# First batch of an attention, gated-MLP and expert-attention kernel: half a q/k tile behind packed scores and weights, bias split earlier, w_o conversion later

## The chip, the cores and the metric

The kernel runs on one core of a Trainium2 chip. The metric is device time in microseconds (us), the median of a few executions. TensorE (PE) does the matmuls, VectorE (DVE), ScalarE (ACT) and GpSimd (POOL) the elementwise work, and SyncE (SP) issues nearly all DMAs.

## The reference

Three stages follow each other for each of 8 batches of 576 tokens.

```python
p_packed = sm_attn(p, k, v)               # 32 packed queries a head, 8 heads, head_dim 64
attn = sm_attn(q, p_packed, p_packed)     # 576 queries a head over the 32 packed rows
x = attn.transpose(0, 2, 1, 3).reshape(B, S, 512)
h = gelu(x @ w_in); u, v = split(h)       # 512 and 512 columns
v_n = layernorm(v) * g_ln
v_s = w_sg @ v_n + b_sg                   # over the 576 tokens
x = x + (u * v_s) @ w_out
# experts: 4 heads of 64 with causal attention, each weighted by a top-2 gate
out = sum_e gate_e(x) * softmax(causal(x wq_e (x wk_e)^T)) (x wv_e) wo_e
```

## The kernel before

**Precision.** Most matmuls run three times (`PASSES`) on operands split into a high and a low part. `act_copy` makes a high part on ACT, `lo_part` the low one on DVE or POOL, both by helpers, so that all of them stand on L83 and L86.

**Two folds.** `w_out` is multiplied into the expert weights (`fold`), so q and k of the experts are made from two sources: the gated part `g` against the folded `w_qk` (`qk_gated`, 24 matmuls a tile), and the attention's own output, whose packed rows are first multiplied with `w_qk` and `w_vg` head by head (`bdw_qk`, `bdw_vg`: 16 matmuls each, giving `bdq` and `bdv`) and then used by `qk_packed` and `vlog`. The weights for `bdw_qk` and `bdw_vg` are other copies than the folded ones: they come by DMA from `kept_qk` and `kept_vg` (L204, L197).

**Order.** `startup()` runs a list of names, `ORDER`, that prepares the weights and the first batch; all engines follow that list there. In it `Dbias` loads `b_sg`, `bi` (`bias_high`, one ACT copy) and `bj` (`bias_low`, four DVE instructions, L304 to L308) split it. After it come, for the first batch, `first_back(0)` and the rest of the batch's second half, then batch by batch a front (MLP) beside the back of the batch ahead. PE and SP take their instructions in the order in which the program writes them. DVE and ACT are placed by a scheduler, except within `manual_schedule` blocks.

**The next batch's keys.** `join("k", j)` interleaves two 16-bit planes (`kp`, loaded from `turned_k`) into a key tile `kT`, two POOL copies for each of four tiles. `make_pT` (L467) transposes the packed queries; `s0` and `s1` are the packed scores (L398), each followed by an exp (`a`, L501). `a0`, `a1` transpose the results (a1T), `pp` multiplies them with v, `P0`, `P1` copy the transposed packed rows (ppT, L446) for the second attention (s with qT, L398), whose result meets `w_in` (wp).

**w_o.** `load_w_o` (L360) loads the experts' output weights; `prep_w_o` converts them, one ACT copy (L83) and one DVE instruction for each of two halves. It is written in `later_back(1)`, and the scheduler places it in the first batch.

Of the kernel before, what the change touches and what calls it, by code (L numbers as in the profile page):

```python
# [26 lines left out]
def packed_attention_mlp_moe_kernel(  # L27
# [18 lines left out]
    nc = tc.nc  # L46
# [44 lines left out]
    ET = mybir.EngineType  # L91
# [293 lines left out]
    STEP = {}  # L385
# [62 lines left out]
    def p1_steps(b):  # L448
# [39 lines left out]
        def join(name, j):  # L488
            t = s.pop((name + "p", j))
            o = slot("D", name=name + "T")  # L490
            w = o.bitcast(U16).rearrange("p (n i) -> p i n", i=2)
            for i in range(2):
                nc.gpsimd.tensor_copy(w[:, i], t[:, i].rearrange("p h n -> p (h n)"))  # L493
            s[name, j] = two(o)

        def s1(Q):
# [67 lines left out]
        last = None  # L564
        for name, src in (("k", k), ("q", q)):
            for j in range(4):
                TURN.append([lambda a=last: a and keep(*a), lambda a=(name, src, j): turn(*a)])
                last = (name, j)
# [14 lines left out]

        STEP[b, "f"] = f_
        if b == 1:
            STEP[b, "fk"], STEP[b, "fv"] = fk_, fv_

        def K(Q):
            if Q == 0:
                make_pT()  # L590
            for j in (2 * Q, 2 * Q + 1):
                join("k", j)
                planes("q", j)

        def Q_(Q):
# [85 lines left out]
    def bdw_qk(b):  # L681
        s = ST[b]
        pt = pd("bdq")
        per_head(b, pt, 512, w_of(b, "qk"))
        for Q in range(2):
            s["bd", Q] = [slot("B", F32R, 512, name="bdq") for _ in range(2)]
            nc.scalar.activation(s["bd", Q][0], pt[:, Q, :], AF.Copy)
        for Q in range(2):
            hi, lo = s["bd", Q]
            lo_part(nc.vector, lo, pt[:, Q, :], hi)  # L690

    def bdw_vg(b):
# [103 lines left out]
    def two(t):  # L796
        return t.rearrange("p (h n) -> p h n", h=2)
# [80 lines left out]
        qk_gated(b, i, True)  # L878
        qk_packed(b, i, False)

    def qk_gated(b, i, first, ms=range(4)):
        s = ST[b]
        if first:
            s["qkp", i] = pd("qk")[:, :, :HALF]
        o = s["qkp", i]
        cols = slice(i * P, (i + 1) * P)
        for m in ms:
            for x, y in PASSES:
                for h in range(2):
                    nc.tensor.matmul(o[:, h, :], W["w_qk"][y][:, m, cols], s["g", m][x][:, hs(h)],  # L890
                                     start=first and (m, x, y) == (0, 0, 0), stop=not first and (m, x, y) == (3, 1, 0))

    def qk_packed(b, i, first):
        s = ST[b]
# [10 lines left out]
    def qk_out(b, i):  # L905
        qk_high(b, i)
        qk_low(b, i)
# [526 lines left out]
    def first_back(b, do_all):  # L1434
        tick(len(TURN))
        do_all("V K0")
        qk_gated(b, 0, True)
        do_all("K1")
        with tc.manual_schedule(engines={ET.DVE}):
            do_all("s0 s1")  # L1440
            bdw_qk(b)
            do_all("n0 n1")
            qk_gated(b, 2, True)
            qk_packed(b, 0, False)
            do_all("a0 a1")
            qk_out(b, 0)
            bdw_vg(b)
            weights(b + 1, ("in1", "in0"))
            qk_packed(b, 2, False)
            qk_out(b, 2)  # L1450
        keep_last_q(b, 0)
        gate_beside(b)
        do_all("pp Q0 Q1")
        vlog(b, VT[2])
        do_all("P0 P1")
        vlog(b, VT[1])
        second(b + 1, do_all)
        load_w_o()
        ahead(b + 2)

    def later_back(b, go, do_all, nxt):
        with tc.manual_schedule(engines={ET.DVE}):
            go("N0 N2")
            vs_tile(b, 0)
        vs_mm(b, 1)
        with tc.manual_schedule(engines={ET.Activation}):
            go("T0 T2")
            vs_out(b, 1)
        vs_tile(b, 2)
        go("y0 y1")  # L1470
        if b == 1:
            for j in range(2):
                prep_w_o(j)
        go("S5 S4")
        vs_tile(b, 3)
        tick(len(TURN))
        if b + 1 < B:
            STEP.pop((b + 1, "f"))()
        with tc.manual_schedule(engines={ET.DVE, ET.Activation}):
            go("o0 T5 T4 o1 y2")  # L1480
            bdw_vg(b)
            bdw_qk(b)
            go("E6 E7 N6 N7")
        weights(b + 1, ("in1", "in0"))
        qk(b, 0)
        do_all("V o2 T6 T7 K0 S8 S9 K1")
        keep_last_q(b, 0)
        gate_beside(b)
        qk_gated(b, 2, True)
        qk_packed(b, 2, False)  # L1490
        qk_high(b, 2)
        with tc.manual_schedule(engines={ET.DVE}):
            do_all("s0 s1")
# [12 lines left out]
    def back(b, go):
        def do_all(names):

            for n in names.split():
                if (b + 1, n) in STEP:  # L1510
                    STEP.pop((b + 1, n))()
                elif n[0] in "STyo":
                    go(n)

        nxt = attention(b)
        if b:
            later_back(b, go, do_all, nxt)
        else:
            first_back(b, do_all)
        if b + 1 == B:  # L1520
            return
        vlog(b, VT[0])
        tick()
        gates(b)
        qk_packed(b, 1, True)
        qk_packed(b, 3, True)
        qk_gated(b, 1, False)
        qk_out(b, 1)
        keep_last_q(b, 1)
        tick()  # L1530
        qk_gated(b, 3, False)
        tick()
        qk_out(b, 3)
        weights(b + 1, ("qk", "vg"))
        return nxt

# [4 lines left out]
    def first():  # L1541
# [189 lines left out]
        for c in range(4):  # L1731
# [10 lines left out]
            Dwsg=lambda: [load_w_sg(c) for c in range(NT)])  # L1742
# [24 lines left out]
        for m in range(4):  # L1767
            for n, fn in (("vk", vs_keep), ("u", u_mm), ("ug", u_gelu), ("go", gate_mul), ("gh", gate_high), ("gl", gate_low)):
                Z[f"{n}{m}"] = lambda fn=fn, m=m: fn(0, m)
        put(ki1=lambda: keep_w_in(1), ki0=lambda: keep_w_in(0), A=lambda: ahead(1), t=tick,  # L1770
            F=lambda: STEP.pop((1, "fk"))(), Fv=lambda: STEP.pop((1, "fv"))(), Wq=load_first_qk,
            W=lambda: weights(0, ("vg",)))
        for i, (o, x) in enumerate(keep_w_steps()):
            Z[f"kw{i}"] = lambda o=o, x=x: nc.sync.dma_start(o, x)
# [1 line left out]

    ORDER = """
        Dwo3 Dwo1 wo3t wo3p Dwo0 Din12 wo1t Dk1 wo3L K1 wo1a wo1p in12t in12a wo1L Kc1 wo0t wo1g Dwo2 wo0p wo2t Dk0
        wo3a wo3g K0 Dp wo0a pT pTc wo0L in12p Dwsg s1 wo0g Din10 in12l Kc0 sm1 se1 wo2p in12g w3 s0 Dq1 ar1 Din13
        sm0 wh3 wv3 aT1 aTc1 se0 Qn1 in10t Dv1 wo2a n1 aT0 Qc1 in10p in13t wo2l w2 wo2g w0 in13p pp1 wH2 aTc0 in13l  # L1780
        n0 wH0 Dq0 ppc1 ppT1 ppTc1 wT1 wL2 S1 Dv0 ar0 wTc1 in10a Qn0 wL0 pp0 in13a St1 Sx1 in10l in13g Din11 wl3 Qc0
        ppc0 in10g in11t wT3 wTc3 in11p w1 ppT0 wT2 w4 Ss1 Dfqk ppTc0 in11l S0 wTc2 Se1 St0 Su1 in11a Sx0 Ss0 wH4
        Dfvg Din00 wh1 Sn1 wv1 Sb1 fa1 ah1 fb1 in11g Se0 wL4 A wp1 fh1 Su0 Sn0 t Sb0 fa2 kw0 wph1 al1 in00t ah0 al0
        Din02 kw1 t wT0 wpl1 fl1 Dbias Dgbc Din03 kw2 v0 Din01 v1 in03t in02t wTc0 t in03p kw3 v2 in03a bi g1 in03l
        g0 bj kw4 in00a wl1 b0 fb2 ki1 b1 kw5 v3 c0 fh2 t in02p pw1 in02a kw6 g2 pw0 c1 b2 g3 in02l vh0 kw7 t pw2
        vh1 c2 kw8 vh2 in03g v4 vl0 b3 fa0 c3 t x4 fb0 fl2 kw9 fh0 in00p y4 vl1 kw10 fl0 pw3 in00l t vl2 g4 b4 vs1_0
        c4 kw11 pw4 vs0_0 vs1_1 vs0_1 vs3_0 vs3_1 in02g vH3 t in01t vs0_2 vs1_2 kw12 vs2_0 vL3 vs3_2 vH4 in01a vL4
        in01p kw13 vs0_3 t vs0_4 in00g in01L vk0 vs3_3 kw14 in01g vs2_1 vs2_2 ki0 wp0 kw15 wph0 vs2_3 vs1_3 kw16
        vs3_4 vs1_4 wpl0 vs2_4 kw17 vk2 u2 u0 ug2 kw18 go2 ug0 go0 u1 kw19 u3 gh2 ug1 F Wq Fv gh0 fa3 gl2 gl0 fb3 W vk1
        go1 vk3 ug3 go3 gh1 gh3 gl1 gl3 fh3 fl3  # L1790
    """

    def startup():
# [42 lines left out]
```

## Time and profile before

| | |
|---|---|
| median of three runs | 797.6 us (797.13 to 800.81) |
| profiled execution, own time | 800.65 us |
| span of its instructions | 798.9 us |
| mean granted PE clock | 0.994 |
| PE / DVE / ACT / POOL busy | 97% / 73% / 53% / 28% |
| DMA moved | 114.05 MB, 143 GB/s |

The profiled execution is 3.05 us above the median. Its time holds 1.75 us beyond the span. Positions below are us from the start of the span. `startup()` reaches to about 98 us, and the first batch's back, with most of the change in it, to about 142 us.

### The profile page before, as it was taken

The numbers are of one execution on the slowest core, as the hardware profiler recorded it, in microseconds if no ns is written. First come the engines' busy times: TensorE is split into PE (matmuls) and PEld (weight loads), VectorE is DVE, ScalarE is ACT, GpSimd is POOL, SyncE is SP. The second block draws the span as 40 slices with busy tenths as digits, with TensorE's granted clock in tenths as the row PEclk, the third lists the DMA queues.
The fourth block names the chain that finished last, engine by engine and source line by source line (L and its number), as shares of the span: only waits on it lengthen the run. The fifth ranks groups of instructions, "written<-read, shape, count | busy, mean of one in ns | idle before, by whom it ended". The sixth has DMA issues, their size and how long they took to land.

```text
span 798.9 us, 18875 instructions
## 1 busy us (share of the span) xinstructions
PE 772.3 (97%) x7361; PEld 682.8 (85%) x7361; DVE 580.2 (73%) x1316; ACT 425.6 (53%) x949; POOL 220.8 (28%) x337
## 2 busy tenths in 40 slices
PE   3899998999999999999999999999999999999998
PEld 1567887998899888998799898998899898998987
DVE  7699447876588767886588766886589676886493
ACT  3665424665347553666357463666347563566365
POOL 1346242315232332304232332304232331400000
PEclk9899999999999999999999999999999999999999
DMA  9997899528382656629283655619273562001002
GB/s 291 263 243 183 190 295 196 144 66 259 68 204 75 196 142 163 156 61 264 76 201 83 160 171 164 161 47 269 66 208 96 130 195 101 1 2 41 1 15 66
DMA packets 169268, 114.05 MB, mean 143 GB/s; under 512 B 115738, under 2 KB 150042, under 8 KB 166492
## 3 DMA queue, kind: packets, MB, share of 16 engines
q1 hardware_dynamic: 169180, 112.86, 53.5%
q8 instruction: 58, 0.95, 0.5%
q14 instruction: 30, 0.25, 0.1%
HBM read 68.26 MB, written 29.63 MB: 123 GB/s over the span
## 4 chain that ended last, share of the span: by engine, by line
PE 89%; DMA 5%; DVE 3%; SPq 1%; issue 1%; ACT 0%; DVEq 0%; ACTq 0%
PE vs L836 13%; PE qk L890 13%; PE qk L902 6%; PE u L806 6%; PE y L1222 6%; PE vlog L963 5%; PE o L1271 5%; PE v L716 5%; PE aTp L1176 3%; PE sc L1047 3%; PE vlog L967 3%; PE s L398 2%; DMA raw_in<-in_moe_w_in_dram 2%; PE wp L636 2%; PE sc L1135 2%; PE sc L1078 1%
## 5 line engine op out<-in xcount | busy, mean ns | idle before, releaser
L890 PE MATMUL qk<-g,w_qk 128*128 128x288 f32 x768 | 107.0, 297 | 0.4 <-ACT a L501 0.4
L890 PEld LDWEIGHTS qk<-g,w_qk 128*128 128x128 f32 x768 | 103.2, 188 | 4.1 <-issue 2.7
L836 PE MATMUL vs<-w_sg,vnh 128*128 128x288 f32 x512 | 90.9, 299 | 1.0 <-DVE w_vg L86 1.0
L836 PEld LDWEIGHTS vs<-w_sg,vnh 128*128 128x128 f32 x512 | 74.6, 188 | 4.8 <-issue 2.1
L1066 ACT ACTIVATE at<-sc,nm 128x384 f32<-128x384 f32 (+3 forms) x72 | 43.3, 607 | 41.6 <-DVE nm L1055 38.8
L83 ACT ACTIVATE aT<-aTp 128x512 f32<-128x512 f32 (+4 forms) x125 | 54.6, 514 | 17.5 <-PE aTp L1106 12.4
L932 POOL CAST g<-g 128x64 fp32r<-128x64 f32 x32 | 10.0, 316 | 168.9 <-DVE g L86 126.3
L836 PE MATMUL vs<-w_sg,vnl 128*128 128x288 f32 x256 | 54.8, 296 | 0.2 <-POOL vnl L86 0.2
L1222 PEld LDWEIGHTS y<-aT,v 128*64 128x64 f32 (+1 forms) x960 | 45.1, 137 | 10.0 <-issue 3.6
L1222 PE MATMUL y<-aT,v 128*64 128x128 f32 (+2 forms) x960 | 52.0, 259 | 0.0
L963 PE MATMUL vlog<-w_vg,g 128*128 128x260 f32 x384 | 52.0, 284 | 0.0
L752 POOL TENSOR_TENSOR rstd<-rstd,mhalf 128x1 f32<-128x1 f32 (+1 forms) x40 | 35.2, 882 | 60.2 <-DVE rstd L748 50.3
L963 PEld LDWEIGHTS vlog<-w_vg,g 128*128 128x128 f32 x384 | 48.4, 189 | 1.1 <-PE wp L636 0.9
L1271 PE MATMUL o<-w_o,y 128*128 128x512 f32 x186 | 48.9, 399 | 0.0
L493 POOL COPY qT<-qp 128x576 uint16<-128x576 uint16 x56 | 44.8, 868 | 13.6 <-DMA qp<-turned_q 13.5
L493 POOL COPY kT<-kp 128x576 uint16<-128x576 uint16 x56 | 43.3, 842 | 14.2 <-PE sc L1047 8.3
L86 DVE TENSOR_TENSOR y<-y 128x256 fp32r<-128x256 f32 (+1 forms) x40 | 15.8, 396 | 42.7 <-ACT y L1248 42.3
L902 PE MATMUL qk<-a2h,bdq 128*128 128x288 f32 x256 | 44.6, 296 | 0.0
L912 ACT ACTIVATE qk<-qk 128x576 fp32r<-128x576 f32 x32 | 20.8, 651 | 41.9 <-PE qk L890 22.0
L836 PEld LDWEIGHTS vs<-w_sg,vnl 128*128 128x128 f32 x256 | 41.1, 188 | 0.4 <-POOL vnl L86 0.4
L927 POOL CAST last_q<-qk 64x64 fp32r<-64x64 f32 x64 | 14.9, 232 | 94.6 <-ACT aT L83 40.4
L548 POOL TENSOR_TENSOR bt<-bt,mx 128x576 f32<-128x576 f32 x14 | 16.2, 1159 | 86.8 <-DVE mx L547 86.8
(267 smaller groups left out, 1916.4 us busy)
## 6 DMA issues: line engine op xcount, KB each, us to landing
w_in<-kept_in SPq DMA_DIRECT2D x14, 1024.0 KB, 7.2
turned_k<-kx SPq DMA_DIRECT2D x28, 288.0 KB, 2.6
turned_q<-qx SPq DMA_DIRECT2D x28, 288.0 KB, 2.4
kp<-turned_k SPq DMA_DIRECT2D x56, 144.0 KB, 3.0
qp<-turned_q SPq DMA_DIRECT2D x56, 144.0 KB, 3.1
out_dram<-ot SPq DMA_DIRECT2D x31, 256.0 KB, 2.1
v<-in_v_dram SPq DMA_DIRECT2D x56, 128.0 KB, 4.7
w_qk<-kept_qk SPq DMA_DIRECT2D x7, 1024.0 KB, 6.6
```

The source lines that it names most:

```text
L83: nc.scalar.activation(o, i, AF.Copy, scale=scale)
L493: nc.gpsimd.tensor_copy(w[:, i], t[:, i].rearrange("p h n -> p (h n)"))
L716: nc.tensor.matmul(pt, s["a2", Q][x][:, c * P:(c + 1) * P], wp_part(b, 1, y, Q), start=n == 0, stop=n == 5)
L752: nc.gpsimd.tensor_tensor(rstd, rstd, mhalf[:TOK[c]], op=OP.pow)
L806: nc.tensor.matmul(pt[:, h, :], wp_part(b, 0, y, Q)[:, m * P:(m + 1) * P], s["a2", Q][x][:, hs(h)], start=n == 0, stop=n == 5)
L836: nc.tensor.matmul(pt[:, h, :], s["vn", c][x][:, cols], w_sg[y][:, c, hs(h)], start=(c, x, y) == (0, 0, 0), stop=False)
L890: nc.tensor.matmul(o[:, h, :], W["w_qk"][y][:, m, cols], s["g", m][x][:, hs(h)], start=first and (m, x, y) == (0, 0, 0), stop=not first an ...
L902: nc.tensor.matmul(o[:, h, :], s["bd", Q][y][:, cols], s["a2", Q][x][:, hs(h)], start=first and (Q, x, y) == (0, 0, 0), stop=not first and ...
L963: nc.tensor.matmul(pt[:, ci, :260], s["g", m][x][:, c * P:c * P + P], W["w_vg"][y][:, m, :], start=(m, x, y) == (0, 0, 0), stop=False)
L1066: nc.scalar.activation(ats[e][:, :L], pt[:, e, :L], AF.Exp, bias=nm[:, e:e + 1], accum_out=sm[:, e:e + 1])
L1222: nc.tensor.matmul(pt[64 * e:64 * e + 64, pr * w:pr * w + w], s["v2"][:m, c, col:col + D], s["aT", pr, e, j][c][:m, :], start=start, stop= ...
L1271: nc.tensor.matmul(pt, ys[:, pr, x, :], W["w_o"][y][:, pr, :], start=i == 0, stop=i == 5)
```

## The change

It has four parts. The bias load and split stand earlier in `ORDER`. The next batch's key joins of batch 1 (the one prepared in `startup`) all stand at the end of `ORDER` as `J`, ahead of `make_pT`, and in two of them one plane is copied by ACT in place of POOL. In `first_back` the first q/k tile's matmuls are cut in two halves, with the packed scores and `bdw_qk` between them, and `bdw_vg` follows right behind. `prep_w_o` stands at the end of the first batch's back, within a block in which ACT and DVE keep to program order too.

```diff
@@ join
             for i in range(2):
-                nc.gpsimd.tensor_copy(w[:, i], t[:, i].rearrange("p h n -> p (h n)"))
+                plane = t[:, i].rearrange("p h n -> p (h n)")
+                if b == 1 and name == "k" and j >= 2 and i == 1:
+                    act_copy(w[:, i], plane)
+                else:
+                    nc.gpsimd.tensor_copy(w[:, i], plane)
@@ steps of batch 1
+        def J():
+            for j in range(4):
+                join("k", j)
         def K(Q):
...
             for j in (2 * Q, 2 * Q + 1):
-                join("k", j)
+                if b > 1:
+                    join("k", j)
                 planes("q", j)
@@ qk_gated
-    def qk_gated(b, i, first, ms=range(4)):
+    def qk_gated(b, i, first, ms=range(4), last=None):
+        last = not first if last is None else last
@@ first_back
         do_all("V K0")
-        qk_gated(b, 0, True)
+        qk_gated(b, 0, True, range(2))
         do_all("K1")
         with tc.manual_schedule(engines={ET.DVE}):
             do_all("s0 s1")
             bdw_qk(b)
+            qk_gated(b, 0, False, range(2, 4), False)
+            bdw_vg(b)
             do_all("n0 n1")
             qk_gated(b, 2, True)
             qk_packed(b, 0, False)
             do_all("a0 a1")
             qk_out(b, 0)
-            bdw_vg(b)
@@ later_back
-        if b == 1:
-            for j in range(2):
-                prep_w_o(j)
@@ end of the back
-        qk_out(b, 3)
+        with tc.manual_schedule(engines={ET.DVE, ET.Activation}):
+            qk_out(b, 3)
+            if b == 0:
+                for j in range(2):
+                    prep_w_o(j)
@@ ORDER
-... w3 s0 Dq1 ar1 Din13 ... Qc1 in10p in13t ... fl1 Dbias Dgbc ... in03a bi g1 in03l g0 bj kw4 ... fh3 fl3
+... w3 s0 Dq1 ar1 Dbias Din13 ... Qc1 in10p bi bj in13t ... fl1 Dgbc ... in03a g1 in03l g0 kw4 ... fh3 fl3 J
```

On PE, in the first batch's back (qk<-g is `qk_gated`, s the packed scores, bdq and bdv the two `bdw`), the order before was:

```order
L890 MATMUL qk<-g,w_qk_589 128x288 x2
L398 MATMUL s_1199<-kT,pT 32x288 x8
L398 MATMUL s_1212<-kT,pT 32x288 x8
L636 MATMUL bdq<-w_qk_1085,ppT 32x512
...
L890 MATMUL qk<-g,w_qk_589 128x288 x2
...
L517 MATMUL a1T<-ident,a_1223 128x128 x4
L518 MATMUL a1T<-ident,a_1223 64x128
L636 MATMUL bdv<-w_vg,ppT 32x260 x8
L902 MATMUL qk<-a2h,bdq 128x288 x4
```

And of the change, at the same place:

```order
L900 MATMUL qk<-g,w_qk_598 128x288 x2
L398 MATMUL s_1187<-kT,pT 32x288 x8
L398 MATMUL s_1200<-kT,pT 32x288 x8
L645 MATMUL bdq<-w_qk_1085,ppT 32x512
...
L900 MATMUL qk<-g,w_qk_598 128x288 x2
L900 MATMUL qk<-g,w_qk_599 128x288 x2
L900 MATMUL qk<-g,w_qk_598 128x288 x4
L900 MATMUL qk<-g,w_qk_599 128x288 x2
L900 MATMUL qk<-g,w_qk_598 128x288 x2
L645 MATMUL bdv<-w_vg,ppT 32x260 x8
L900 MATMUL qk<-g,w_qk_598 128x288 x2
```

Twelve of the 24 matmuls of the first tile now stand behind bdq, and bdv stands ahead of the second tile's 24 matmuls, of the eight of `qk_packed` and of the ten a1T transposes, all of which it followed before.

On SP, the DMA issues at the same place (v, vrest and qp are the next batch's, w_vg is what bdv reads) were:

```order
L204 DMA w_qk_1087<-kept_qk 128x1024
L375 DMA v<-in_v_dram 128x4x64 x4
L381 DMA vrest<-in_v_dram 64x4x64 x2
L375 DMA v<-in_v_dram 128x4x64
L197 DMA w_vg<-kept_vg 128x1040
L375 DMA v<-in_v_dram 128x4x64 x3
```

And they are:

```order
L204 DMA w_qk_1087<-kept_qk 128x1024
L375 DMA v<-in_v_dram 128x4x64 x4
L381 DMA vrest<-in_v_dram 64x4x64 x2
L375 DMA v<-in_v_dram 128x4x64 x3
L197 DMA w_vg<-kept_vg 128x1040
L375 DMA v<-in_v_dram 128x4x64
```

The load of w_vg has two more v loads ahead of it.

On ACT, from the last fold copy to the copies of the packed rows (L446), the rows were:

```order
L83 ACTIVATE w_vg_591<-fold 128x260
L83 ACTIVATE pT<-pT 128x256
L501 ACT_TABLE_LOAD
...
L697 ACTIVATE bdv<-bdv 128x520
L912 ACTIVATE qk<-qk 128x576
L83 ACTIVATE w_o_1566<-wst_1568 128x512
L974 ACTIVATE v_1410<-vlog 64x256
L446 ACTIVATE ppT<-ppT 128x128 x2
```

And they are, with those at the end of the batch (from `qk<-qk x2` on) behind the second mark:

```order
L83 ACTIVATE w_vg_600<-fold 128x260
L83 ACTIVATE kT<-kp 128x576 x2
L83 ACTIVATE pT<-pT 128x256
L505 ACT_TABLE_LOAD
...
L706 ACTIVATE bdv<-bdv 128x520
L922 ACTIVATE qk<-qk 128x576 x2
L984 ACTIVATE v_1410<-vlog 64x256
L446 ACTIVATE ppT<-ppT 128x128 x2
...
L922 ACTIVATE qk<-qk 128x576 x2
L83 ACTIVATE w_o_1566<-wst_1568 128x512
L83 ACTIVATE w_o_1566<-wst_1570 128x512
L83 ACTIVATE vg<-v 64x512
```

Two key copies stand ahead of the copy of pT, no w_o copy stands ahead of L446 any more, and both w_o copies stand ahead of the next batch's `vg<-v`.

## Rows read from the trace of the kernel before

**Rows 1.** Waits of PE, whole span: total us, times, longest.

```profile
PE s L398 <- ACT ppT L446: 2.6, 1, 2.6
PE vs L836 <- DVE w_vg L86: 1.0, 1, 1.0
```

**Rows 2.** Timeline of PE, first batch: start, us, work, [idle before <- releaser].

```profile
98.36 3.42 PE L890 MATMUL qk<-g,w_qk 128*128 128x288 f32 x24
101.71 1.20 PE L398 MATMUL s<-kT,pT 64*32 64x288 f32 x32
102.70 1.06 PE L636 MATMUL bdq<-w_qk,ppT 64*32 64x512 f32 x16
104.21 3.46 PE L890 MATMUL qk<-g,w_qk 128*128 128x288 f32 x24 [0.44 <-ACT a L501]
...
110.83 0.67 PE L636 MATMUL bdv<-w_vg,ppT 64*32 64x260 f32 x16 [0.47 <-PE a1T L518]
...
123.36 1.94 PE L398 MATMUL s<-qT,ppT 64*32 64x288 f32 x32 [2.60 <-ACT ppT L446]
124.95 3.03 PE L636 MATMUL wp<-w_in,ppT 64*32 64x512 f32 x32
```

**Rows 3.** Timeline of ACT at the two places of the change in that stretch.

```profile
98.86 0.38 ACT L83 ACTIVATE w_vg<-fold 128x260 fp32r<-128x260 f32 x1
99.12 0.39 ACT L83 ACTIVATE pT<-pT 128x256 f32<-128x256 f32 x1
...
121.88 0.63 ACT L83 ACTIVATE w_o<-wst 128x512 fp32r<-128x512 f32 x1 [7.91 <-DMA wst<-in_moe_wo_dram]
122.54 0.38 ACT L974 ACTIVATE v<-vlog 64x256 f32<-64x256 f32 x1
122.94 0.45 ACT L446 ACTIVATE ppT<-ppT 128x128 f32<-128x128 f32 x2
```

**Rows 4.** Windows of 1 us: busy PE, PEld, DVE, ACT, POOL; granted clock; DMA share, GB/s.

```profile
122.00:123.00 1.00, 0.00 (x0) 0.00 (x0) 0.46 (x1) 0.95 (x3) 0.00 (x0) 1.00 0.34 40
...
126.00:127.00 1.00, 1.00 (x24) 0.45 (x15) 1.00 (x3) 0.00 (x0) 0.43 (x1) 0.50 2.33 135
127.00:128.00 1.00, 1.00 (x18) 0.10 (x1) 0.94 (x2) 0.23 (x1) 0.73 (x1) 0.95 0.60 15
```

**Rows 5.** Timeline of SP's issues around the load of w_vg.

```profile
99.28 3.48 SPq L381 DMA_DIRECT2D vrest<-in_v_dram  x2
...
103.50 0.45 SPq L197 DMA_DIRECT2D w_vg<-kept_vg  x1
104.00 2.45 SPq L375 DMA_DIRECT2D v<-in_v_dram  x3
```

**Rows 6.** DMA issues, 88 to 126 us: count, KB each, median us from issue to landing.

```profile
kp<-turned_k SPq DMA_DIRECT2D x8, 144.0 KB, 4.4
...
w_vg<-kept_vg SPq DMA_DIRECT2D x1, 520.0 KB, 4.8
```

**Rows 7.** DMA, same stretch: busy tenths and GB/s in 40 slices.

```profile
DMA  9944547999999999997999999999799999993409
```

**Rows 8.** Timeline of POOL, the key joins of the first batch.

```profile
96.05 6.10 POOL L493 COPY kT<-kp 128x576 uint16<-128x576 uint16 x8 [4.36 <-DMA kp<-turned_k]
```

**Rows 9.** Timeline of DVE in startup: the bias's new place, then its old one.

```profile
28.92 0.43 DVE L157 TENSOR_SCALAR w_in<-raw_in 128x512 int32<-128x512 int32 x1 [3.10 <-DMA raw_in<-in_moe_w_in_dram]
...
57.72 1.38 DVE L307 TENSOR_SCALAR bh<-bh,sel 2x576 f32<-2x576 f32 x1
59.13 1.73 DVE L308 SCALAR_TENSOR_TENSOR w_sg<-bb,sel,bh 2x576 fp32r<-2x576 f32 x1
```

**Rows 10.** Timeline of ACT where the next batch's front begins.

```profile
143.08 0.59 ACT L83 ACTIVATE vg<-v 64x512 f32<-64x512 f32 x1 [0.28 <-PE v L711]
```

**Rows 11.** Timeline of DVE where that front's expert attention is normed.

```profile
163.49 1.38 DVE L1096 TENSOR_SCALAR at<-at,sm,gw 128x256 f32<-128x256 f32 x4
```

**Rows 12.** Timeline of PE at the same place.

```profile
163.86 1.50 PE L1106 MATMUL aTp<-ident,at 128*128 128x128 f32 x12
165.15 0.79 PE L836 MATMUL vs<-w_sg,vnh 128*128 128x288 f32 x4
```

More of the change, by code (lines that the diff above doesn't have):

```diff
@@ L585, in p1_steps @@
         if b == 1:
-            STEP[b, "fk"], STEP[b, "fv"] = fk_, fv_
+            STEP[b, "fk"], STEP[b, "fv"], STEP[b, "J"] = fk_, fv_, lambda: J()
+        def J():
+            for j in range(4):
+                join("k", j)
         def K(Q):
@@ L890, in qk_gated @@
                     nc.tensor.matmul(o[:, h, :], W["w_qk"][y][:, m, cols], s["g", m][x][:, hs(h)],
-                                     start=first and (m, x, y) == (0, 0, 0), stop=not first and (m, x, y) == (3, 1, 0))
+                                     start=first and (m, x, y) == (0, 0, 0), stop=last and (m, x, y) == (3, 1, 0))
     def qk_packed(b, i, first):
@@ L1770, in first @@
         put(ki1=lambda: keep_w_in(1), ki0=lambda: keep_w_in(0), A=lambda: ahead(1), t=tick,
-            F=lambda: STEP.pop((1, "fk"))(), Fv=lambda: STEP.pop((1, "fv"))(), Wq=load_first_qk,
+            F=lambda: STEP.pop((1, "fk"))(), Fv=lambda: STEP.pop((1, "fv"))(), J=lambda: STEP.pop((1, "J"))(),
+            Wq=load_first_qk,
             W=lambda: weights(0, ("vg",)))
@@ L1778, in packed_attention_mlp_moe_kernel @@
         Dwo3 Dwo1 wo3t wo3p Dwo0 Din12 wo1t Dk1 wo3L K1 wo1a wo1p in12t in12a wo1L Kc1 wo0t wo1g Dwo2 wo0p wo2t Dk0
-        wo3a wo3g K0 Dp wo0a pT pTc wo0L in12p Dwsg s1 wo0g Din10 in12l Kc0 sm1 se1 wo2p in12g w3 s0 Dq1 ar1 Din13
-        sm0 wh3 wv3 aT1 aTc1 se0 Qn1 in10t Dv1 wo2a n1 aT0 Qc1 in10p in13t wo2l w2 wo2g w0 in13p pp1 wH2 aTc0 in13l
+        wo3a wo3g K0 Dp wo0a pT pTc wo0L in12p Dwsg s1 wo0g Din10 in12l Kc0 sm1 se1 wo2p in12g w3 s0 Dq1 ar1 Dbias Din13
+        sm0 wh3 wv3 aT1 aTc1 se0 Qn1 in10t Dv1 wo2a n1 aT0 Qc1 in10p bi bj in13t wo2l w2 wo2g w0 in13p pp1 wH2 aTc0 in13l
         n0 wH0 Dq0 ppc1 ppT1 ppTc1 wT1 wL2 S1 Dv0 ar0 wTc1 in10a Qn0 wL0 pp0 in13a St1 Sx1 in10l in13g Din11 wl3 Qc0
@@ L1783, in packed_attention_mlp_moe_kernel @@
         Dfvg Din00 wh1 Sn1 wv1 Sb1 fa1 ah1 fb1 in11g Se0 wL4 A wp1 fh1 Su0 Sn0 t Sb0 fa2 kw0 wph1 al1 in00t ah0 al0
-        Din02 kw1 t wT0 wpl1 fl1 Dbias Dgbc Din03 kw2 v0 Din01 v1 in03t in02t wTc0 t in03p kw3 v2 in03a bi g1 in03l
-        g0 bj kw4 in00a wl1 b0 fb2 ki1 b1 kw5 v3 c0 fh2 t in02p pw1 in02a kw6 g2 pw0 c1 b2 g3 in02l vh0 kw7 t pw2
+        Din02 kw1 t wT0 wpl1 fl1 Dgbc Din03 kw2 v0 Din01 v1 in03t in02t wTc0 t in03p kw3 v2 in03a g1 in03l
+        g0 kw4 in00a wl1 b0 fb2 ki1 b1 kw5 v3 c0 fh2 t in02p pw1 in02a kw6 g2 pw0 c1 b2 g3 in02l vh0 kw7 t pw2
         vh1 c2 kw8 vh2 in03g v4 vl0 b3 fa0 c3 t x4 fb0 fl2 kw9 fh0 in00p y4 vl1 kw10 fl0 pw3 in00l t vl2 g4 b4 vs1_0
@@ L1789, in packed_attention_mlp_moe_kernel @@
         vs3_4 vs1_4 wpl0 vs2_4 kw17 vk2 u2 u0 ug2 kw18 go2 ug0 go0 u1 kw19 u3 gh2 ug1 F Wq Fv gh0 fa3 gl2 gl0 fb3 W vk1
-        go1 vk3 ug3 go3 gh1 gh3 gl1 gl3 fh3 fl3
+        go1 vk3 ug3 go3 gh1 gh3 gl1 gl3 fh3 fl3 J
     """
```

## The prediction

> **What bounds the kernel now.** The table of engines comes first: PE is busy 97% of the span, so the time is the length of PE's stream plus the holes in it. The list of waits says where the holes are. Two of them lie at work that the change touches: 2.6 us ahead of the second attention's scores, put down to ACT's copies of the packed rows, and 1.0 us ahead of a `vs` tile in startup, put down to DVE [rows 1]. What comes off or on between holes elsewhere counts only if PE waits for it.
>
> The timeline of PE in the first batch is where most of the change acts [rows 2]. From 98.36 us PE runs a q/k tile (24 matmuls), packed scores, bdq, a hole of 0.44, the second tile's gated part and what follows, a hole of 0.47, bdv, and more until the hole of 2.60 that ends at 123.36; 32 score matmuls and the 32 of wp follow until 124.95 + 3.03 = 127.98. The timeline of ACT shows what the 2.60 is: ACT stood 7.91 us at a w_o copy, for that weight's DMA, and the two copies of the packed rows started only at 122.94, behind it [rows 3]. So it is a load that PE waits for there, through ACT's program order.
>
> That hole cost more than its length. The granted clock was 1.00 in the microsecond of the hole, 0.50 in the one from 126 and 0.95 in the one from 127: the lower level, 1.2 GHz, then back [rows 4]. Priced by the same forms at full clock, the scores take 102.70 - 101.71 = 0.99 us per 32, and 16 per-head matmuls of bdq take 1.06, so 32 take 2.1: together 3.1 us. They took 127.98 - 123.36 = 4.6 [rows 2]. The lower clock cost 1.5.
>
> **What the change removes.** The holes of 0.44 (bdv and half a tile now cover the exp) and 0.47 (bdv no longer stands behind the transposes), the 2.60 (no w_o copy ahead of the packed rows' copies any more; the v copy of 0.38 at 122.54 stays ahead of them, but its input is ready when vlog ends) and the 1.5 of the clock: 5.0 us in all. Bounds: 4.4 if the copies still end 0.6 behind PE, and 5.0.
>
> **What the first batch gets in their place.** I follow PE from 98.36. Half a tile is 12 of 24 matmuls; 24 took 101.71 - 98.36 = 3.35, so PE comes to the packed scores at 100.0. They need pT's copy, which now stands behind two key copies on ACT. ACT ends its last fold copy at 98.86 + 0.38 = 99.24; a copy of 512 elements a row took 0.63, I take 0.6 each for 576, and 0.39 for pT [rows 3]: 100.85. POOL's share is no later: 8 copies took 6.10 from 96.05, six take 4.6 and end at 100.6 [rows 8]. PE waits about 0.85 (bounds 0.4, one key copy hidden, and 2.0, when the planes land late: such a load took 4.4 us from its issue [rows 6]). Then scores 0.99, bdq 1.06, half a tile 1.7: PE stands at bdv at 104.6.
>
> Now bdv needs w_vg. Before, that load was issued at 103.50 and took 4.8 us, so it landed at 108.3, while bdv started only at 110.83 [rows 2, 5, 6]: 2.5 us of slack. The change wants it 6 us earlier and issues it later: two more v loads stand ahead of it on SP, and three of them took 2.45 us, 0.8 each [rows 5]. The queue can't catch up, since nearly every slice of the DMA line from 95 us on reads 9 [rows 7]. Issue at 103.5 + 1.6 = 105.1 with 4.8 behind it gives 109.9; with the cheaper of the three v issues, or some catching up, 109.3. I take 109.6, and bound it by 108.3 (as before) and 110.9 (the two loads cost as much again in transfer). So PE waits 109.6 - 104.6 = 5.0 us (3.7 to 6.3), and behind it in its order stand the second tile, both packed parts and the transposes, which need no w_vg. On PE nothing can pass.
>
> A hole of 5.0 is longer than the one of 2.60 behind which the clock fell, so I count the clock's price again: 1.5 by that row, up to 2.9 if it grows with the hole (1.5 x 5.0 / 2.6), taken as 1.8, near the row, because the clock came back by itself after some 3.5 us of work [rows 4]. [...]
>
> **The w_o conversion at its new place.** It hides nothing there: ACT does two w_o copies of 0.6 right ahead of the next batch's `vg<-v`, which started at 143.08 after 0.28 us idle [rows 3, 10]. That idle time takes up 0.3, and ACT's chain runs 0.9 later through gelu, normalisation and the exps to the DVE norm at 163.49, 0.35 us for each quarter [rows 11]. PE's transposes of it start at 163.86, 0.02 after the first quarter, with other matmuls around them [rows 12]. So a late norm is a hole. ACT also waits for other engines in between, where delay is lost: bounds 0 and 0.9, taken 0.8. The two DVE parts run beside it.
>
> **The bias.** Its two long DVE instructions took 1.38 and 1.73, with two short ones of about 0.15 some 3.4 us [rows 9]. At the old place DVE was late for the `vs` tile at 70 us that waited 1.0 [rows 1]; leaving gains at most that. At the new place DVE waited 3.10 us for a DMA [rows 9], which covers most of it; without that cover it costs up to 3.4. So -1.0 to +3.4 in startup. I cost it at nothing: whether PE reaches bdv at 103.6 or 108.0, it leaves at 109.6, because the w_vg load hangs on SP's issues. The new wait swallows it, as it swallows the 0.85 for pT as soon as that grows: the two are one hole, 5.85 in all, ended by the landing.
>
> **Sum.** -5.0 (holes and clock removed) + 0.85 + 5.0 (pT and w_vg) + 1.8 (clock) + 0.8 (w_o) = +3.4 us. The profiled execution would have 798.9 + 3.4 = 802.3 of span and 800.65 + 3.4 = 804.0 of own time. It stood 3.05 above the median, so the median goes from 797.6 to 801.0. Adding the low bounds (-5.0 + 0.85 + 3.7 + 1.5 + 0) gives +1.0; a landing at 110.9 and the rest as taken give +4.7, and with 2.6 for the clock +5.5.
>
> **Rivals.** A measurement here tells a change from none from about 0.5%, 4.0 us.
> - *Same hole, clock kept.* The clock row shows one fall behind one hole; PE was at 1.00 all through the hole itself [rows 4]. If it doesn't fall behind bdv: -5.0 + 0.85 + 5.0 + 0.8 = +1.6, and with a landing at 108.3 +0.3 (or -0.5 without w_o's part). Chance 0.22.
> - *w_vg comes in time: faster.* Two vrest issues held SP for 3.48 us [rows 5]. If the v issues and that stretch shrink, so that w_vg lands by 104.6, the wait and its clock price go: -5.0 + 0.85 + 0.8 = -3.4, or -4.2 with w_o hidden. The side turns at a landing of about 106.2, where wait (1.6) and clock (1.8) eat the gain. It needs an issue at 101.4, and the row says 103.50 with fewer loads ahead. Against it: the busy DMA line [rows 7]. Chance 0.08.
> - *Late loads spread.* Loads that wait for buffers which PE frees, w_o among them, slide with PE, and with them the loads behind them on SP. If the next batch meets them as ACT met w_o (7.91 of waiting), it pays up to the hole's 5.0 once more: +5 to +9. For it: SP is in program order. Against: with the change no w_o copy stands ahead of what PE waits for in that batch [rows 3]. Chance 0.08.
>
> **How the numbers follow.** The forecast's own case, +1.0 to +5.5, has 0.62. The range 797.5 to 804.5 (-0.1 to +6.9) holds it, most of the second case and the lower half of the last: about 0.87; the faster case stays out. Slower by over 4.0: the upper part of the forecast (0.28 of the 0.62) and the last rival, 0.36. Faster by over 4.0: half of the w_vg rival, 0.04. The rest, 0.60, is within.
>
> **What would show it.** In the profile after: a wait of bdv for w_vg's DMA of about 5 us, ended near 109.6, with the clock at 0.50 behind it; no wait of 2.60 at the second scores, and no ACT wait for w_o ahead of L446; packed scores at about 100.85; a small new wait of aTp near 165 on DVE. The prediction is wrong if w_vg lands early, if bdv's hole costs no clock, or if startup moves by more than 5 us, so that the hole no longer covers it.

## The result and the profile after

The changed kernel takes 804.57 us, the median of 804.08 to 805.09, against 798.01 for the kernel before: a ratio of 1.0078, 95% interval [1.0064, 1.0093], slower by 6.6 us. The forecast of 801.0 was 3.6 us short, and slower by over 0.5% had been given 0.36 against 0.60 for within. The +6.6 lies above the forecast's own case (+1.0 to +5.5) and just inside the whole range (-0.1 to +6.9). In the trace the sum came out almost exactly: +3.5 us of span (798.9 to 802.4), own time 804.10 where 804.0 was forecast; how much of that is luck is told below. So there are two questions: where the time went, and why the medians lie 3.1 us further apart than the two profiled executions.

The list of PE's waits in the changed kernel, from its second row on (total us, times, longest), answers to [rows 1]; the first row is the wait for k's load at the start, 11.5:

```profile
PE bdv L645 <- DMA w_vg<-kept_vg: 4.7, 1, 4.7
PE ppT L441 <- DVE pp L436: 2.7, 1, 2.7
PE wsgT L256 <- DMA wst<-in_moe_w_sg_dram: 1.5, 1, 1.5
PE s L398 <- POOL g L942: 1.5, 1, 1.5
...
PE qk L912 <- DVE sm L560: 0.4, 1, 0.4
...
PE aTp L1116 <- DVE at L1106: 0.3, 1, 0.3
```

The 2.6 at the second scores and the 1.0 at the `vs` tile are gone. The largest wait behind the start's is new, and it is bdv's. The timeline of PE in the first batch, beside [rows 2]:

```profile
96.83 1.82 PE L900 MATMUL qk<-g,w_qk 128*128 128x288 f32 x12
100.17 1.20 PE L398 MATMUL s<-kT,pT 64*32 64x288 f32 x32 [1.52 <-POOL g L942]
101.13 1.86 PE L645 MATMUL bdq<-w_qk,ppT 64*32 64x512 f32 x16
102.92 1.85 PE L900 MATMUL qk<-g,w_qk 128*128 128x288 f32 x12
109.49 0.89 PE L645 MATMUL bdv<-w_vg,ppT 64*32 64x260 f32 x16 [4.72 <-DMA w_vg<-kept_vg]
110.31 4.74 PE L900 MATMUL qk<-g,w_qk 128*128 128x288 f32 x24
...
126.75 1.20 PE L398 MATMUL s<-qT,ppT 64*32 64x288 f32 x32
127.74 1.92 PE L645 MATMUL wp<-w_in,ppT 64*32 64x512 f32 x32
```

PE comes to half a tile 1.53 us earlier than before (96.83 for 98.36), stands ready for bdv at 104.8 and leaves at 109.49. Then bdv and the 24 matmuls take 0.82 + 4.58 = 5.40 us (the next row starts at 114.89), where the same work took 0.60 + 3.29 = 3.9 at full clock in the kernel before (from each row's start to the next one's). Farther down, the second scores follow vlog without a gap and run at full speed; wp ends at 129.66, where it ended at 127.98: +1.7 from the start of the span. SP's issues, beside [rows 5]:

```profile
98.95 3.26 SPq L381 DMA_DIRECT2D vrest<-in_v_dram  x2
102.31 2.41 SPq L375 DMA_DIRECT2D v<-in_v_dram  x3
104.82 0.45 SPq L197 DMA_DIRECT2D w_vg<-kept_vg  x1
105.31 0.43 SPq L375 DMA_DIRECT2D v<-in_v_dram  x1
```

Issue at 104.82, use at 109.49: 4.7 us from the one to the other. Windows of 1 us (columns as in [rows 4]) show the clock at the end of the wait:

```profile
108.00:109.00 1.00, 0.00 (x0) 0.00 (x0) 0.00 (x0) 0.00 (x0) 0.00 (x0) 1.00 1.16 291
109.00:110.00 1.00, 0.51 (x16) 0.21 (x16) 0.00 (x0) 0.00 (x0) 0.00 (x0) 0.91 1.19 189
110.00:111.00 1.00, 1.00 (x11) 0.69 (x4) 0.00 (x0) 0.48 (x1) 0.00 (x0) 0.50 1.21 237
...
113.00:114.00 1.00, 1.00 (x9) 1.00 (x8) 0.00 (x0) 0.00 (x0) 0.00 (x0) 0.89 1.59 316
```

In the window from 108 no engine does anything but DMA. The clock is 0.50 from 110 to 113 and then comes back: 5.40 - 3.9 = 1.5 us lost.

### The profile page after: what moved, and what is told of

Its sections match the earlier page's. It is cut to its first block, busy times and chain, and to the rows that moved or that the text cites. A ratio compares the mean times of both kernels' runs of the same rounds, so it can differ in the third digit from the quotient of the medians.

```text
span 802.4 us, 18867 instructions
## 1 busy us (share of the span) xinstructions
PE 773.1 (96%) x7361; PEld 683.2 (85%) x7361; DVE 576.1 (72%) x1316; ACT 427.0 (53%) x951; POOL 219.0 (27%) x335
## 4 chain that ended last, share of the span: by engine, by line
PE 82%; DMA 8%; DVE 4%; SPq 3%; ACT 2%; issue 1%; POOL 0%; POOLq 0%; ACTq 0%; DVEq 0%
PE qk L900 13%; PE vs L845 11%; PE qk L912 6%; PE y L1232 6%; PE vlog L973 5%; PE o L1281 5%; PE u L815 5%; PE v L725 4%; PE aTp L1186 3%; PE sc L1057 3%; PE vlog L977 3%; DMA qx<-in_q_dram 2%; PE s L398 2%; PE sc L1145 1%; PE wp L645 1%; PE aTp L1116 1%
```

## The experiments

Each ratio is to the kernel before, run on the same chip; the interval is 95%.

| run | median us | before | ratio |
|---|---|---|---|
| e1 before again | 798.56 | 798.73 | 1.0004 [0.9992, 1.0015] |
| e2 w_vg load first | 797.34 | 798.73 | 0.9981 [0.9972, 0.9990] |
| e3 bdv at its old place | 798.21 | 798.73 | 0.9991 [0.9981, 1.0002] |
| e4 w_o alone | 799.05 | 798.73 | 1.0007 [0.9997, 1.0016] |
| e5 second tile ahead of bdv | 799.32 | 798.63 | 1.0009 [0.9995, 1.0022] |
| e6 wait filled | 802.26 | 798.63 | 1.0048 [1.0036, 1.0060] |
| e7 e2 with w_o later | 796.75 | 798.63 | 0.9973 [0.9963, 0.9982] |
| e8 bias at its old place | 799.26 | 798.63 | 1.0006 [0.9996, 1.0016] |
| e9 load order of before | 800.72 | 798.24 | 1.0031 [1.0016, 1.0046] |
| e10 e8 with the change's load order | 800.32 | 798.24 | 1.0028 [1.0013, 1.0043] |
| e11 before, w_o later | 798.26 | 798.24 | 0.9994 [0.9980, 1.0008] |
| e12 bias alone | 798.48 | 798.24 | 1.0007 [0.9994, 1.0020] |

### Is it the wait of bdv? (e2, e3)

e2 takes the loads out of `ORDER` and writes w_vg ahead of all v loads:

```diff
-... F Wq Fv gh0 fa3 gl2 gl0 fb3 W vk1
+... F Wq gh0 fa3 gl2 gl0 fb3 vk1
         tick(len(TURN))
-        do_all("V K0")
+        weights(b, ("vg",))
+        do_all("fv V K0")
```

> The changed kernel with the load of w_vg issued ahead of all eight v loads and vrest. Theory (bdv's wait for w_vg and the clock behind it are the loss): w_vg is issued near 97 and lands near 102, bdv starts at about 104.6 with no wait over 0.5 us, the clock stays at 1.00, and 4.7 us of wait and about 1.4 of clock go: 804.6 - 6.1 = 798.5, ratio to before 1.000. Rival (the loss lies in the w_o copies, the split tile or startup): the wait goes but the time stays above 802, ratio 1.005 or more.

e3 leaves the loads and puts the matmuls back:

```diff
             qk_gated(b, 0, False, range(2, 4), False)
-            bdw_vg(b)
...
             qk_out(b, 0)
+            bdw_vg(b)
```

> The changed kernel with bdw_vg back behind the transposes of a1T; the load order is that of the change. Theory (the place of bdv is what makes the load late): no wait of bdv above 0.6 us, since it starts at about 110 while w_vg lands at 109.5; 804.6 - 5.5 to 6.1 = 798.5 to 799.1, ratio 1.001. Rival (the loss lies elsewhere): above 802, ratio 1.005 or more.

Both undo the loss: 797.34 and 798.21. In e2, the timelines of SP and of PE, then PE's of e3:

```profile
97.56 0.38 SPq L197 DMA_DIRECT2D w_vg<-kept_vg  x1
```

```profile
105.58 0.67 PE L645 MATMUL bdv<-w_vg,ppT 64*32 64x260 f32 x16
```

```profile
111.46 0.67 PE L645 MATMUL bdv<-w_vg,ppT 64*32 64x260 f32 x16 [0.47 <-PE a1T L522]
```

In e2 the load is issued 7.3 us earlier, and bdv has no idle time ahead of it. In e3 w_vg is issued as late as in the change (105.30), but bdv waits only for the transposes. So early bdv and late w_vg make the loss together; either alone is harmless. What e2 and e3 keep of the change is worth -1.4 and -0.5 us; e3's interval includes no change.

### What the clock costs (e5, e6)

e5 moves real work into the wait:

```diff
+            qk_gated(b, 2, True)
             bdw_vg(b)
             do_all("n0 n1")
-            qk_gated(b, 2, True)
```

> The changed kernel with the second q/k tile's 24 gated matmuls moved ahead of bdw_vg; loads as in the change. They take about 3.3 us at full clock and need no w_vg. Theory (the landing of w_vg sets the end, work put ahead of it is free): bdv starts at 109.5 again, its wait is 4.7 - 3.3 = 1.4, too short to cost the clock, so 3.3 + 1.4 = 4.7 us are won: 804.6 - 4.7 = 799.9, ratio to before 1.0015. Rival (PE's own order costs nothing there, the loss is elsewhere): above 802.5, ratio 1.005 or more.

It gives 799.32 where 799.9 was expected. In its profiled execution SP issued w_vg at 101.53, 3.3 us earlier than in the changed kernel, and bdv had no wait left, so the expected wait of 1.4 was not met there. Its times spread over 796.8 to 801.9.

e6 puts useless matmuls there:

```diff
+            fill = pd("fill")
+            for _ in range(34):
+                nc.tensor.matmul(fill[:, 0, :HALF], W["w_qk"][0][:, 0, 0:P], ST[b]["g", 0][0][:, hs(0)], start=True, stop=True)
             bdw_vg(b)
```

> The changed kernel with 34 added matmuls of 128x288 ahead of bdw_vg, into a PSUM buffer that nothing reads; they do no useful work and take 34 x 0.134 = 4.6 us, as long as the wait of bdv. It prices the clock by itself. Theory (the hole costs 4.7 and the clock behind it some 1.4): bdv starts at 109.5 again, with next to no wait, the granted clock stays at 1.00, and the time falls by 1.4 to about 803.2, although PE does more work; ratio to the changed kernel 0.998, to before 1.006. Rival (the clock behind the hole costs nothing on the path, since loads bound what follows): 804.6 or more, ratio to before 1.0075.

The timeline of PE in e6:

```profile
104.57 4.64 PE L1455 MATMUL fill<-g,w_qk 128*128 128x288 f32 x34
109.19 0.67 PE L645 MATMUL bdv<-w_vg,ppT 64*32 64x260 f32 x16
109.79 3.45 PE L900 MATMUL qk<-g,w_qk 128*128 128x288 f32 x24
```

And its windows across the end of the fill:

```profile
108.00:110.00 2.00, 2.00 (x27) 1.40 (x26) 0.00 (x0) 0.00 (x0) 0.00 (x0) 1.00 1.15 239
110.00:112.00 2.00, 2.00 (x16) 2.00 (x16) 1.14 (x5) 0.60 (x1) 0.00 (x0) 1.00 1.14 238
```

PE does 4.6 us more work, waits for nothing at bdv, keeps its clock at 1.00, and the kernel is 2.3 us faster than the changed one (1.8 between the spans of the two profiles, 800.6 and 802.4). Of that, 3.89 us for bdv and the tile against 5.40 is the clock, 1.5, and 0.3 an earlier leave (109.19 for 109.49); the rows don't place the remaining 0.5 of the medians. The wait itself is still paid, as 34 matmuls.

### Why the load is late (e8, e9, e10)

e8 puts the bias back into its old places in `ORDER` and leaves the rest of the change:

```diff
-... ar1 Dbias Din13 ... Qc1 in10p bi bj in13t ... fl1 Dgbc ... in03a g1 in03l g0 kw4
+... ar1 Din13 ... Qc1 in10p in13t ... fl1 Dbias Dgbc ... in03a bi g1 in03l g0 bj kw4
```

> The changed kernel with the bias load and split at their old places in startup. The trace of the change has PE ahead by 1.5 us at 90 us, which bdv's wait swallows. Theory (the landing of w_vg sets the end, startup's gain is lost in the hole): the wait of bdv shrinks from 4.7 to about 3.3 and the time stays within 0.5 us: 804.1 to 805.1, ratio to before 1.0075. Rival (the load is issued later too when startup is longer, since it waits for the fold's buffer): 804.6 + 1.3 = 805.9, ratio 1.009.

Both expectations missed: the bias is worth 5.3 us here, 799.26 for 804.57 (5.7 by the two ratios to the kernel before). SP's timeline of e8, and PE's:

```profile
97.65 3.23 SPq L381 DMA_DIRECT2D vrest<-in_v_dram  x2
100.98 0.55 SPq L375 DMA_DIRECT2D v<-in_v_dram  x1
101.63 0.45 SPq L197 DMA_DIRECT2D w_vg<-kept_vg  x1
102.13 1.53 SPq L375 DMA_DIRECT2D v<-in_v_dram  x3
```

```profile
101.68 1.21 PE L398 MATMUL s<-kT,pT 64*32 64x288 f32 x32 [0.86 <-ACT pT L83]
...
107.02 0.67 PE L645 MATMUL bdv<-w_vg,ppT 64*32 64x260 f32 x16 [1.50 <-DMA w_vg<-kept_vg]
```

With the bias back, w_vg stands behind one v load again. The w_vg load is the last of `startup()`, the v loads are the first of the block behind it. Yet one to three of these v loads stand ahead of w_vg on SP, so SP keeps the written order only within a block; from one block to the next the order is the scheduler's. It was the bias move, some 75 us ahead, that turned the order: e12, which is that move alone, has three v loads ahead of w_vg too. But startup is also different, so two runs hold one and change the other. e9 keeps the early bias and forces the old order (w_vg issued inside `V`, behind its first load):

```diff
-    def load_nat(name, src, b, j, t=None):
+    def load_nat(name, src, b, j, t=None, after=None):
...
             nc.sync.dma_start(t[:, h]..., dap(src, off + h * S * D, ...))
+            if after == h:
+                weights(0, ("vg",))
...
-                load_nat("v", v, b, j, t[:, (j - 2) * 512:(j - 1) * 512])
+                load_nat("v", v, b, j, t[:, (j - 2) * 512:(j - 1) * 512], 0 if (b, j) == (1, 2) else None)
...
-... fb3 W vk1
+... fb3 vk1
```

> The changed kernel, bias early, with the SP order of the kernel before forced: w_vg behind one v load after vrest, not three. Putting the bias back (e8) brought back that order as well as the longer startup, and with both 5.3 us; this run holds startup as it is and moves only the two loads. Theory (the order of the loads is what the bias move cost): issue near 103.0 in place of 104.8, landing near 107.6, a wait of bdv of about 2.9, so 1.9 us less, and 1.4 more where the clock no longer falls: 801.3 to 802.7, ratio to before 1.0035 to 1.005. Rival (order is a trifle; with an early bias, startup itself makes SP late): 804.0 or more, ratio above 1.0065.

e10 is e8 with the same device, behind the third load.

> The converse: the changed kernel with the bias at its old place (e8, 799.3) but the SP order of the change forced, w_vg behind three v loads. Theory (the order of the loads is the cost): w_vg lands 1.2 to 1.9 later than in e8, at 108.2 to 108.9, bdv waits 2.7 to 3.4 in place of 1.5, and at that length the clock may fall: 800.5 to 802.6, ratio to before 1.0025 to 1.005. Rival (the early bias itself was the cost): as e8, 799.3, ratio 1.0006.

e9 wins 3.9 of the 5.3 us, e10 gives back 1.1 (both to their parents in the table; 1.8 for e10 by the two ratios). The rows of bdv in e9, then SP's issue and bdv in e10:

```profile
107.14 0.67 PE L647 MATMUL bdv<-w_vg,ppT 64*32 64x260 f32 x16 [2.89 <-DMA w_vg<-kept_vg]
```

```profile
102.12 1.17 SPq L197 DMA_DIRECT2D w_vg<-kept_vg  x1
```

```profile
106.86 1.12 PE L647 MATMUL bdv<-w_vg,ppT 64*32 64x260 f32 x16 [3.02 <-DMA w_vg<-kept_vg]
```

So with the bias early the order of two v loads is the larger part of what the bias move cost. e10 does not confirm it from the other side: a landing of 108.2 to 108.9 was expected, but in its profile bdv left at 106.86, 0.16 earlier than in e8 with the old order, and what it lost there is the clock, which fell behind the wait of 3.02. Nor do the rows show the part that is left: bdv leaves at 107.14 in e9 and at 107.02 in e8, so an earlier startup only makes the wait longer, and yet the medians lie 1.5 apart. The split is not sharp, because SP's pace differs between executions (w_vg issued at 101.53 in e5 and at 104.82 in the changed kernel, in the same order), and e9's times spread over 797.3 to 803.5.

### What the removed wait was worth (e1, e4, e11, e12)

e4 and e11 move `prep_w_o` alone in the kernel before, e4 as the change does, e11 to a place where ACT waited for PE in the second batch. The edit of e11:

```diff
 later_back
             go("T0 T2")
             vs_out(b, 1)
+            if b == 1:
+                for j in range(2):
+                    prep_w_o(j)
         vs_tile(b, 2)
         go("y0 y1")
-        if b == 1:
-            for j in range(2):
-                prep_w_o(j)
```

> The kernel before with one part of the change, prep_w_o at the end of the first batch's back. Theory (the w_o copy held up the packed rows' copies): the hole of 2.60 and its clock of 1.5 go, 0.8 at most is given back at the next front: 798.0 - 3.3 = 794.7, ratio 0.996. Rival (the hole of 2.60 was special to the long execution that was profiled, and the usual ones had none): no gain, 798.0 to 798.8, ratio 1.000 to 1.001.

> The kernel before with prep_w_o alone moved, to the place of e7 behind vs_out(1), where it was 0.6 cheaper than at the end of the back. Theory now (the hole of 2.60 and its clock, seen in both profiles of the kernel before, are smaller in its usual executions, whose median is 2.2 under the profiled ones): little is won, 798.0 to 798.6, ratio 0.999 to 1.000. Rival (the hole is there in all executions and costs 4.1 each time): 794.6 to 795.2, ratio 0.9955.

> The kernel before, unchanged, profiled a second time. The measured difference of the medians (804.57 against 798.01, +6.6 us) is larger than that of the two profiled executions (804.10 against 800.65, +3.45). Theory (the profiled execution of before was one of its long ones): ratio 1.000 within 0.3%, and this profile has a span of about 796, without part of what the first one lost (the start's loads, the hole of 2.60 or the clock behind it). Rival (the offset between own time and span moves): the span is 798.9 again.

The rows of e1's second scores and wp:

```profile
122.48 2.18 PE L398 MATMUL s<-qT,ppT 64*32 64x288 f32 x32 [3.06 <-ACT ppT L446]
124.38 3.70 PE L636 MATMUL wp<-w_in,ppT 64*32 64x512 f32 x32
```

e1's profile has the wait of the second scores again, 3.1 us with the clock at 0.50 behind it; its span is 799.2 and its own time 800.93, while its median is 798.56. Its rival's number came true, then: this profile is no shorter than the first. Its reason did not: own time less span is 1.75 and 1.73. And yet taking the wait away wins nothing in the medians: 1.0007, as e4's rival had it, and 0.9994, at most 1.6 us by the lower end of e11, where 4.1 less the w_o copies had been credited. In both profiles the wait is gone and PE runs 4.4 us quicker from the start of bdv to the end of wp (17.15 us in the kernel before, 12.76 in e4, 12.77 in e11), but startup is slower in them: bdv starts at 113.08 in e4 and 111.49 in e11, for 110.83. The rows of the `vs` tiles in e11, and its windows:

```profile
68.05 0.53 PE L836 MATMUL vs<-w_sg,vnl 128*128 128x288 f32 x2 [1.39 <-POOL vnl L86]
69.63 0.78 PE L836 MATMUL vs<-w_sg,vnh 128*128 128x288 f32 x4 [1.05 <-DVE w_vg L86]
```

```profile
70.00:76.00 6.00, 6.00 (x36) 6.00 (x36) 5.90 (x12) 2.66 (x5) 4.36 (x5) 0.72 0.92 208
```

PE comes to these tiles 2 us earlier than in the first profile, waits longer for POOL (1.39 for 0.20) and as long for DVE, and the clock falls here. The bias move removes those waits, and e12 is that move alone:

```diff
-... ar1 Din13 ... Qc1 in10p in13t ... fl1 Dbias Dgbc ... in03a bi g1 in03l g0 bj kw4
+... ar1 Dbias Din13 ... Qc1 in10p bi bj in13t ... fl1 Dgbc ... in03a g1 in03l g0 kw4
```

> The kernel before with the bias part of the change alone. It moves w_vg behind three v loads on SP here too, but bdv stands at its old place, at about 110. Theory (startup's gain of about 1.3 is real, and bdv at 109 to 110 has w_vg just in time): 798.6 - 1.3 = 797.3 where the later hole at the packed rows doesn't take it back, 798.6 where it does, ratio 0.998 to 1.000. Rival (the late load costs here too, since PE comes to bdv 1.3 earlier): a wait of bdv of 1 us or more, ratio above 1.001.

Its ratio is 1.0007, no gain. Startup has no wait at the `vs` tiles in it, and PE then waits at the second scores for the w_o copy, as in the kernel before:

```profile
120.94 1.39 PE L398 MATMUL s<-qT,ppT 64*32 64x288 f32 x32 [1.24 <-ACT ppT L446]
```

A reading that fits the medians is that the two waits stand one behind the other on PE: what startup wins is lost at the second scores, whose end w_o's landing sets, and an execution that has lost time in startup has little wait left there. e4, e11 and e12 each remove one of the two, and win nothing; e2, e7 and e3 remove both, and win 1.4, 1.9 and 0.5. But e12's profile does not show it: its second scores start 2.4 us earlier than in the first profile (120.94 for 123.36), and its span of 796.0 keeps that. That the kernel before usually has the first wait and seldom the second is argued from the medians, 2.2 us under the profiled executions.

The mean granted clock, which is known for every execution, gives a hint: both profiled ones of the kernel before read 0.994, while of the 99 others that the runs are compared with the median is 0.996, and only 12 read 0.994 or less. As an estimate, 0.002 of 799 us is 1.6 us of PE's time, about what one fall of the clock cost. So the two profiles are of executions that stood longer at the lower clock than usual ones. Which of the waits the usual ones lack no profile shows, so that stays open.

### A version that beats both (e7)

e7 is e2 with `prep_w_o` at the place of e11.

> The kernel with the load of w_vg ahead of the v loads (797.3, ratio 0.998) and in it prep_w_o moved from the end of the first batch's back to a place in the next one where ACT waited 2.15 us for PE, behind vs_out(1). Theory (the two w_o copies push the next front's chain by 0.8 at most): the wait of aTp for the norm (0.28) goes, and something of the slope from 131 to 162 us (0.5): 797.3 - 0.5 to 0.8 = 796.5 to 796.8, ratio to before 0.997. Rival (that chain's delay is from elsewhere, such as DVE): the same as e2, 0.998, with the aTp wait still there.

It takes 796.75, ratio 0.9973: 1.9 us under the kernel before, 7.8 under the changed one. Its PE has no wait at bdv, at the second scores or at the first aTp:

```profile
104.64 0.67 PE L645 MATMUL bdv<-w_vg,ppT 64*32 64x260 f32 x16
```

```profile
PE aTp L1186 <- DVE at L1131: 0.3, 1, 0.3
```

The step from e2 (ratio 0.9981) is 0.6 us, about what the w_o copies were taken to cost, but their intervals overlap. Nor does the trace settle it: the wait ahead of the first aTp is gone, but one as long stands ahead of a later aTp (the second view, from the list of waits), which e2 does not have.

## Why the prediction was right and where it was wrong

**w_vg.** Right in place and size. A landing of 109.6 and a wait of 5.0 were forecast; bdv left at 109.49 after 4.72. The slack of 2.5 us in [rows 2, 5, 6] was the reading that decided. The wait's size has some luck in it: PE came 1.53 early to the half tile, and lost that again through 0.67 more than forecast at pT, 0.73 more in bdq (1.79 for 1.06) and 0.3 in the two half tiles.

**The clock.** 1.8 was taken, 1.5 came out, about as much as behind the old wait [rows 4] although the wait was nearly twice as long. By the changed kernel's rows, which have the second scores and wp at full clock (126.75 to 129.66, 2.9 us for 4.6), the old fall cost 1.7, not 1.5. e6 shows that the price is paid for the idle time and not for the late load. The price is not fixed: see the last section. The Trainium skill, page TensorE: Matmul & The Clock Gate, section Why this matters for your kernels, warns of idle gaps between bursts of matmuls above a length that it gives, because TensorE falls back to half its rate behind them. The fall behind 4.72 us agrees; the one behind 2.60 us does not, since that gap is shorter than the length that the Trainium skill gives.

**pT.** 0.85 was taken and 1.52 measured, with a cause beside it: the last key plane landed for POOL only at 99.0. It cost nothing, since bdv's wait followed.

**w_o at its new place.** 0.8 was taken. The trace shows 0.28 at aTp [rows 12], and e7 against e2 says 0.6, within the noise.

**The removed waits.** In the trace they went as forecast, 2.60 with its clock and the two of 0.44 and 0.47. A little came back: 0.45 at the next `qk_packed`, where PE now waits for DVE (`qk <- DVE sm`), as it does in e2, e4, e7 and e11. The term of 5.0 was mis-sized for the median: e4 and e11 put the largest part of it, 4.1, at 1.6 or less. With it fails the step that "the median goes from 797.6 to 801.0" because the profiled execution "stood 3.05 above the median". The profiled execution of the changed kernel lies 0.5 under its own median, and the difference of these two distances is 3.5 of the 3.6 us by which the forecast was short. That the distance was part of what the change removed is argued, not shown.

**The sum.** That +3.4 and +3.5 agree is luck in part. Up to the end of wp the terms give +2.65, and +1.7 was measured; behind it 1.8 was lost where 0.8 had been taken for w_o.

**The bias.** It was "cost at nothing", because bdv leaves when w_vg has landed. That swallowing is in the trace: PE 1.53 ahead at 96.83, and nothing of it left at 109.49. What the step missed is that the bias move itself had put two more v loads ahead of w_vg. The order of SP was read, but its cause was not asked for; e8 gives 5.3 us for the move. The early bias also has a price in startup, which the `vs` tiles more than pay back: PE waits 2.7 us for DVE at the first ppT, for 1.3 before. That wait is 1.2 to 1.4 in every profile with the bias at its old place and 2.2 to 3.2 in every one with it early. The row of the kernel before:

```profile
PE ppT L441 <- DVE pp L436: 1.3, 1, 1.3
```

**The rivals.** The clock fell, against the first. w_vg came late, against the second; e2 is what that rival describes, and it gives -1.4, not -3.4, in line with the mis-sized term of the removed waits. Of late loads spreading nothing is to be seen: behind wp the distance of the two traces grows by 0.6 at the wait for DVE (L560), by 0.5 at aTp and by 0.25 or less at each of a few places up to the end, none of them a wait for a load.

## What to carry to other kernels

Before matmuls move forward, look up when each of their operands lands: slack that a load has behind its user is invisible in a list of waits. A wait that a profile shows can be worth less in the median: the 2.60 us and its clock stood in both profiles, and taking them away won at most 1.6. Compare the profiled execution's time and mean clock with those of the others first; a distance between profile and median need not carry over to the changed kernel. When an edit changes the order on a queue far from its own place, run it alone before it is booked as free.

## What the runs showed of the hardware

The clock behind a wait is not given by the wait's length in these runs. In the first batch it fell behind 2.60 (kernel before), 3.02 (e10), 3.06 (e1) and 4.72 (changed), and did not behind 1.24 (e12), 1.50 (e8) and 2.89 (e9). In startup it fell behind two shorter waits close together, 1.39 and 1.05 (e11, shown above). The windows of e9, then of e10, across and behind nearly equal waits:

```profile
104.00:108.00 4.00, 1.11 (x20) 0.49 (x20) 1.04 (x2) 0.01 (x1) 0.00 (x0) 1.00 0.98 259
108.00:112.00 4.00, 4.00 (x32) 4.00 (x32) 1.14 (x5) 0.59 (x1) 0.00 (x0) 1.00 1.08 229
```

```profile
104.00:108.00 4.00, 1.14 (x17) 0.34 (x17) 1.29 (x2) 0.14 (x1) 0.00 (x0) 0.75 0.96 252
108.00:112.00 4.00, 4.00 (x17) 4.00 (x18) 1.14 (x5) 0.60 (x1) 0.00 (x0) 0.50 1.28 246
```

What a fall costs differs too. It cost 1.5 (changed kernel) and 1.7 (kernel before), where the clock was still 1.00 in the microsecond ahead of the work. It cost 2.7 in e1 (5.6 us for the scores and wp, where the changed kernel took 2.9) and 2.65 in e10 (19.39 us from bdv to wp for e8's 16.74), where the clock fell within the wait: e10's 0.75 is 2 of 4 us at the lower level with 1.14 us of work in them, and e1's microsecond from 121 has 0.83 though its scores start at 122.48.

The two long bias instructions of DVE got shorter by moving: 1.38 and 1.73 us beside a busy POOL [rows 9], 0.51 and 0.81 where POOL did nothing; e1 and e8 repeat the first pair within 0.02, e12 the second. A window of the kernel before, then DVE's timeline of the changed kernel and its window:

```profile
58.00:59.00 1.00, 1.00 (x8) 0.90 (x7) 1.00 (x1) 1.00 (x2) 1.00 (x2) 1.00 1.16 353
```

```profile
28.09 0.51 DVE L307 TENSOR_SCALAR bh<-bh,sel 2x576 f32<-2x576 f32 x1 [1.87 <-ACT bh L83]
28.64 0.81 DVE L308 SCALAR_TENSOR_TENSOR w_sg<-bb,sel,bh 2x576 fp32r<-2x576 f32 x1
```

```profile
28.00:29.00 1.00, 0.31 (x4) 0.17 (x4) 0.87 (x2) 0.96 (x4) 0.00 (x0) 1.00 0.81 237
```

The Trainium skill has a reason for such a stretch, page SBUF — State Buffer, section Who interferes with whom: DVE and GpSimd share one pair of ports, and an instruction that holds it blocks the other engine. The 1.8 us between the two places agree with it; no run here varied POOL alone.
